# All matmuls as 64-row halves in pairs, the convolution in the h ring, turns through SyncE

## The chip, the cores and the metric

The kernel runs on one core of a Trainium2 chip. The metric is device time in microseconds of one execution, lower is better. The engines of the core work side by side, each through its own instructions in order: TensorE (PE) for matmuls, ScalarE (ACT), VectorE (DVE), GpSimd (POOL), and SyncE (SP), which issues most of the DMAs. They wait for each other by semaphores. TensorE writes into PSUM, eight banks of 2 KB per partition; ACT and DVE read it from there.

## The reference

A causal convolution of 7 taps, one softmaxed filter per head of 24 channels, and then a two-layer network with the gate h·cos(h):

```python
w = softmax(weight, axis=-1)                      # [8 heads, 7 taps]
x_pad = zeros(6 tokens) + x                       # x: [8, 4096, 192] float32
out[b,s,h,g] = sum_k w[h,k] * x_pad[b, s+k, h, g]  # 8 heads x 24 channels
x = out.reshape(32768, 192)
h = x @ w_in                                      # [192, 2048]
g = h * cos(h)
return g @ w_out                                  # [2048, 192], float32
```

## The kernel before

The 32768 tokens are worked in 64 tiles `t` of T = 512 tokens; two tiles make a unit `u` of 1024 tokens, the grain of loading, convolution and transposing. All matmuls take bf16 and sum in float32.

Per unit: `load_unit` loads x (SP's DMA queue), `cast_unit` makes it bf16 on POOL, with the block before it in front. `conv_pair` makes the convolution on PE, tokens on the 128 partitions: for each head, one matmul with a 128x128 band of filter taps on the block itself and one on the block before. `conv_out` copies the result to `ct` on ACT. `turn_unit` doubles 64 of the 192 channels on POOL, so that they later stand on both halves of the partitions, and transposes `ct` into `cT` (channels on partitions) by a DMA that SP issues, `dma_start_transpose`.

Per tile there are NP = 8 stages `j`. In stage `j`, `mm1(t, j)` makes 256 of the 2048 hidden features in a tile `h` of two PSUM banks. The contraction of 192 is 128 + 64: two matmuls of 64 rows (`w2`, one on the upper and one on the lower half of the rows, each to its own bank, line 184) and two of 128 rows (`w1`, line 187). ACT takes sin(h + pi/2) into `cs` (line 189) and DVE multiplies `h` by `cs` into `g` (line 192). Then `mm2(t - 1, j)` makes a part of the output of the tile before: 8 of the 64 matmuls `g` times `wo` that the tile needs, of 128 rows and 192 columns (line 204). After every second 128-token block ACT copies `o_ps` to `o_sb` (line 207) and after the fourth SP issues the store (line 209).

There is no scheduler: each engine runs its instructions in the order in which the loops write them (`manual_schedule`). The convolution of the next unit stands in stages 0, 2, 4 and 6 of the even tiles, and `turn_unit`, `load_unit` and `cast_unit` in stage 0 of the odd ones. PSUM: three `h` tiles (six banks), one bank for `o_ps`, one for `c_ps`.

Of the kernel before, what the change touches and what calls it, by code (L numbers as in the profile page):

```python
# [8 lines left out]
FP32 = mybir.dt.float32  # L9
BF16 = mybir.dt.bfloat16  # L10
AF = mybir.ActivationFunctionType
ALU = mybir.AluOpType
PSUM = bass.MemoryType.PSUM
# [3 lines left out]
def kernel(  # L17
# [8 lines left out]
    nc = tc.nc  # L26
    B, S, D = x.shape
    H, K = weight.shape
    Dff = moe_w_in.shape[1]
    G = D // H  # L30
    NTOK = B * S
    T = 512
    NT = NTOK // T
    NB = T // 128
    U = 1024
    NU = NTOK // U
    UB = U // 128
    UPS = S // U
    TPU = U // T
    NF = Dff // 128  # L40
    NP = NF // 2
# [4 lines left out]
    consts = ctx.enter_context(tc.tile_pool(name="consts", bufs=1))  # L46
# [5 lines left out]
    cos_pool = ctx.enter_context(tc.tile_pool(name="cos", bufs=3))  # L52
    gpool = ctx.enter_context(tc.tile_pool(name="g", bufs=2))
    opool = ctx.enter_context(tc.tile_pool(name="o", bufs=2))
    h_pool = ctx.enter_context(tc.tile_pool(name="h_ps", bufs=3, space=PSUM))
    o_pool = ctx.enter_context(tc.tile_pool(name="o_ps", bufs=1, space=PSUM))
    c_pool = ctx.enter_context(tc.tile_pool(name="c_ps", bufs=1, space=PSUM))

    ctx.enter_context(tc.manual_schedule())

# [6 lines left out]
    def load_unit(u):  # L67
        xt = xin.tile([128, UB, D], FP32, name="x_f")
        nc.sync.dma_start(out=xt, in_=xf[u * U : (u + 1) * U, :].rearrange("(n p) d -> p n d", p=128))
        x_tiles[u] = xt  # L70
# [14 lines left out]
    row = consts.tile([H, LR], BF16)  # L85
# [18 lines left out]
    band = consts.tile([128, H, 256], BF16)  # L104
    nc.vector.tensor_copy(out=band, in_=skew[:, :, ::-1])  # L105

    halfpi = consts.tile([128, 1], FP32)
    nc.vector.memset(halfpi, math.pi / 2.0)  # L108

    w1 = consts.tile([128, Dff], BF16)  # L110
    w2 = consts.tile([128, NP, 128], BF16)
    wo = consts.tile([128, NF, D], BF16)


    prev = {}
    bf = {}

    def cast_unit(u):
        xt = x_tiles.pop(u)
        xb = xbf_pool.tile([128, UB + 1, D], BF16, name="x_bf")  # L120
        if u % UPS == 0:
            nc.gpsimd.memset(xb[:, 0, :], 0.0)  # L122
        else:
            nc.gpsimd.tensor_copy(out=xb[:, 0, :], in_=bf[u - 1][:, UB, :])  # L124
        nc.gpsimd.tensor_copy(out=xb[:, 1 : UB + 1, :], in_=xt)  # L125
        bf[u] = xb
        bf.pop(u - 2, None)

    ct_tiles = {}

    def conv_pair(u, q):

        xb = bf[u]
        if q == 0:
            ct_tiles[u] = ct_pool.tile([128, UB, 256], BF16, name="ct")
        ct = ct_tiles[u]
        ps = c_pool.tile([128, 2, UB, G], FP32, name="c_ps")
        for i in range(2):
            h = 2 * q + i
            hs = slice(h * G, (h + 1) * G)  # L140
            nc.tensor.matmul(out=ps[:, i], lhsT=band[:, h, 0:128], rhs=xb[:, 1 : UB + 1, hs], start=True, stop=False)  # L141
            nc.tensor.matmul(out=ps[:, i], lhsT=band[:, h, 128:256], rhs=xb[:, 0:UB, hs], start=False, stop=True)  # L142
        return ct, ps

    def conv_out(q, ct, ps):
        o = ct[:, :, 2 * q * G : (2 * q + 2) * G].rearrange("p n (i g) -> p i n g", i=2)
        nc.scalar.copy(o, ps)  # L147

    cT = {}

    def turn_unit(u):
        ct = ct_tiles.pop(u)
        nc.gpsimd.tensor_copy(out=ct[:, :, D:256], in_=ct[:, :, 128:D])  # L153
        t = cT_pool.tile([128, UB, 2, 128], BF16, name="cT")
        nc.sync.dma_start_transpose(out=t.rearrange("p n c k -> p (n c) k"), in_=ct.rearrange("p n k -> p (n k)"))
        cT[u] = t
        cT.pop(u - 2, None)

    def conv_unit(u):
        for q in range(H // 2):  # L160
            conv_out(q, *conv_pair(u, q))
        turn_unit(u)

    cast_unit(0)
    nc.gpsimd.tensor_copy(out=w2, in_=w2_f)  # L165
    nc.vector.tensor_copy(out=w1, in_=w1_f)
    conv_unit(0)
    cast_unit(1)
    for q in range(4):
# [3 lines left out]
    g_tiles = {}  # L173
    o_state = {}

    def mm1(t, j):

        c = cT[t // TPU]
        n0 = (t % TPU) * NB
        x1 = c[:, n0 : n0 + NB, 0, :]  # L180
        h = h_pool.tile([128, 2, T], FP32, name="h")
        for i in range(2):
            r = slice(64 * i, 64 * i + 64)
            nc.tensor.matmul(out=h[:, i, :], lhsT=w2[r, j, :], rhs=c[r, n0 : n0 + NB, 1, :], start=True, stop=False)  # L184
        for i in range(2):
            f = 2 * j + i
            nc.tensor.matmul(out=h[:, i, :], lhsT=w1[:, f * 128 : (f + 1) * 128], rhs=x1, start=False, stop=True)  # L187
        cs = cos_pool.tile([128, 2, T], BF16, name="cs")
        nc.scalar.activation(out=cs, in_=h, func=AF.Sin, bias=halfpi, scale=1.0)  # L189
        if j == 0:  # L190
            g_tiles[t] = gpool.tile([128, NF, T], BF16, name="g")
        nc.vector.tensor_tensor(out=g_tiles[t][:, 2 * j : 2 * j + 2, :], in0=h, in1=cs, op=ALU.mult)  # L192

    def mm2(t, j):

        g = g_tiles[t]
        s, half = divmod(j, 2)
        if s % 2 == 0 and half == 0:
            o_state["ps"] = o_pool.tile([128, 2, 256], FP32, name="o_ps")
        if j == 0:  # L200
            o_state["sb"] = opool.tile([128, NB, D], FP32, name="o_sb")
        ps, sb = o_state["ps"], o_state["sb"]
        for f in range(half * 8, half * 8 + 8):
            nc.tensor.matmul(out=ps[:, s % 2, 0:D], lhsT=g[:, f, s * 128 : (s + 1) * 128], rhs=wo[:, f, :],  # L204
                             start=(f == 0), stop=(f == NF - 1))
        if s % 2 == 1 and half == 1:
            nc.scalar.copy(sb[:, s - 1 : s + 1, :], ps[:, :, 0:D])  # L207
            if s == NB - 1:
                nc.sync.dma_start(out=out[t * T : (t + 1) * T, :].rearrange("(n p) d -> p n d", p=128), in_=sb)

    for t in range(NT + 1):
        u_next = t // TPU + 1
        for j in range(NP):
            if t < NT:
                mm1(t, j)
                if u_next < NU:
                    k = (t % TPU) * NP + j
                    if k < H and k % 2 == 0:
                        conv_out(k // 2, *conv_pair(u_next, k // 2))
                    if k == H:  # L220
                        turn_unit(u_next)
                        if u_next + 1 < NU:
                            load_unit(u_next + 1)
                            cast_unit(u_next + 1)
            if t > 0:
                mm2(t - 1, j)


# [28 lines left out]
```

## Time and profile before

| | |
|---|---|
| time, median of 3 runs | 874.5 us (874.49 to 874.55) |
| the profiled execution | 874.82 us, span 873.0 us, granted clock 1.0 |
| PE matmuls of 64 rows, `h`, L184 | 1024 x 388 ns |
| PE matmuls of 128 rows, `h`, L187 | 1024 x 385 ns |
| PE matmuls, `o_ps`, L204 | 4096 x 246 ns |
| ACT sine L189, copies L147 and L207 | 512 x 1114 ns, 128 x 472 ns, 128 x 472 ns |
| DVE multiply L192 | 512 x 1225 ns |
| POOL cast L125, halo copy L124, doubling L153 | 1468 ns, 350 ns, 616 ns |
| x load and transpose, issue to landing | 4.9 us, 5.0 us |

A line of the groups names the source line, the engine, the operation, what is written and read, its count, and then the busy time, the mean of one instruction in ns, and the idle time before them with what ended it. A matmul's recorded time runs from its start to the end of its way through the array, so records of one stream overlap: the interval between starts tells what a matmul costs in a stream. In a timeline each row has the start, the time covered, the engine and what ran; neighbours of one kind are merged (x8).

### The profile page before, as it was taken

The numbers are of one execution on the slowest core, as the hardware profiler recorded it, in microseconds if no ns is written. First come the engines' busy times: TensorE is split into PE (matmuls) and PEld (weight loads), VectorE is DVE, ScalarE is ACT, GpSimd is POOL, SyncE is SP. The second block draws the span as 40 slices with busy tenths as digits, with TensorE's granted clock in tenths as the row PEclk, the third lists the DMA queues.
The fourth block names the chain that finished last, engine by engine and source line by source line (L and its number), as shares of the span: only waits on it lengthen the run. The fifth ranks groups of instructions, "written<-read, shape, count | busy, mean of one in ns | idle before, by whom it ended". The sixth has DMA issues, their size and how long they took to land.

```text
span 873.0 us, 15646 instructions
## 1 busy us (share of the span) xinstructions
PE 835.6 (96%) x6656; PEld 504.3 (58%) x6656; DVE 631.7 (72%) x525; ACT 668.0 (77%) x771; POOL 76.5 (9%) x101
## 2 busy tenths in 40 slices
PE   0699999999999999999999999999999999999997
PEld 0256566665656665556666566665656666556655
DVE  1477777777777777777777777777777777777774
ACT  0577878877778787778777778778777887777874
POOL 1101100101100101110101110100110110110000
PEclk9999999999999999999999999999999999999999
DMA  8133332133332133333134333124334223334201
GB/s 241 24 80 97 86 90 62 58 93 97 96 81 70 59 85 97 98 79 77 59 78 98 97 79 89 53 71 98 97 80 88 59 66 97 97 80 97 57 25 54
DMA packets 138038, 71.80 MB, mean 82 GB/s; under 512 B 68200, under 2 KB 137840, under 8 KB 137840
## 3 DMA queue, kind: packets, MB, share of 16 engines
q1 hardware_dynamic: 136896, 70.27, 31.5%
q8 instruction: 52, 0.85, 0.4%
q10 hardware_dynamic: 1072, 0.53, 0.2%
q14 instruction: 18, 0.15, 0.1%
HBM read 28.84 MB, written 25.17 MB: 62 GB/s over the span
## 4 chain that ended last, share of the span: by engine, by line
PE 84%; ACT 7%; issue 5%; DMA 2%; DVE 0%; POOL 0%; ACTq 0%
PE o_ps L204 35%; PE h L187 27%; PE h L184 16%; ACT o_sb L207 4%; ACT cs L189 3%; PE c_ps L141 3%; PE c_ps L142 2%; DMA skew<-row_d 1%; DMA row_d<-row 1%; DMA cT<-ct 0%; DVE g L192 0%; ACT ct L147 0%; DMA w_sb<-in_weight_dram 0%; ACT L91 0%; DVE band L105 0%
## 5 line engine op out<-in xcount | busy, mean ns | idle before, releaser
L192 DVE TENSOR_TENSOR g<-h,cs 128x1024 bf16<-128x1024 f32 x512 | 626.9, 1225 | 213.5 <-ACT cs L189 213.4
L189 ACT ACTIVATE cs<-h,halfpi 128x1024 bf16<-128x1024 f32 x512 | 570.1, 1114 | 173.5 <-PE h L187 169.0
L204 PE MATMUL o_ps<-wo,g 128*128 128x192 bf16 x4096 | 420.4, 246 | 4.9 <-ACT o_sb L207 1.5
L204 PEld LDWEIGHTS <-g 128*128 128x128 bf16 x4096 | 351.4, 98 | 106.7 <-issue 23.5
L187 PE MATMUL h<-cT,w 128*128 128x512 bf16 x1024 | 310.9, 385 | 0.0
L184 PE MATMUL h<-cT,w 64*128 64x512 bf16 x1024 | 200.5, 388 | 6.4 <-DMA cT<-ct 5.6
L187 PEld LDWEIGHTS <-w 128*128 128x128 bf16 x1024 | 57.9, 97 | 116.5 <-issue 116.5
L184 PEld LDWEIGHTS <-w 64*128 64x128 bf16 x1024 | 49.6, 93 | 88.6 <-issue 88.5
L147 ACT CAST ct<-c_ps 128x384 bf16<-128x384 f32 x128 | 60.4, 472 | 20.1 <-PE c_ps L142 20.1
L141 PE MATMUL c_ps<-x_bf,band 128*128 128x192 bf16 x256 | 53.8, 250 | 22.0 <-DVE halfpi L108 20.3
L125 POOL CAST x_bf<-x_f 128x1536 bf16<-128x1536 f32 x32 | 47.0, 1468 | 299.6 <-DMA x_f<-in_x_dram 299.6
L207 ACT COPY o_sb<-o_ps 128x384 f32<-128x384 f32 x128 | 60.4, 472 | 5.8 <-PE o_ps L204 5.8
L153 POOL COPY ct<-ct 128x512 bf16<-128x512 bf16 x32 | 19.7, 616 | 443.2 <-ACT ct L147 443.2
L142 PE MATMUL c_ps<-x_bf,band 128*128 128x192 bf16 x256 | 54.0, 251 | 0.0
L141 PEld LDWEIGHTS <-band 128*128 128x128 bf16 x256 | 25.6, 100 | 35.4 <-DVE halfpi L108 20.3
L142 PEld LDWEIGHTS <-band 128*128 128x128 bf16 x256 | 25.4, 99 | 17.3 <-issue 2.9
L105 DVE COPY band<-skew 128x2048 bf16<-128x2048 bf16 x1 | 0.7, 694 | 15.2 <-DMA skew<-row_d 15.2
L124 POOL COPY x_bf<-x_bf 128x192 bf16<-128x192 bf16 x24 | 8.4, 350 | 0.0
L91 ACT ACT_TABLE_LOAD x1 | 1.3, 1283 | 2.2 <-DMA w_sb<-in_weight_dram 2.2
L122 POOL MEMSET x_bf<- 128x192 bf16 x8 | 2.1, 259 | 0.3 <-POOLq L241 0.3
L170 DVE CAST wo<-wo_f 128x768 bf16<-128x768 f32 x4 | 2.0, 554 | 0.0
L165 POOL CAST w<-w_f 128x1024 bf16<-128x1024 f32 x1 | 1.0, 1042 | 4.0 <-DMA w_f<-in_moe_w_in_dram 4.0
(14 smaller groups left out, 4.3 us busy)
## 6 DMA issues: line engine op xcount, KB each, us to landing
x_f<-in_x_dram SPq DMA_DIRECT2D x32, 768.0 KB, 4.9
out_dram<-o_sb SPq DMA_DIRECT2D x64, 384.0 KB, 2.9
wo_f<-in_moe_w_out_dram SPq DMA_DIRECT2D x1, 1536.0 KB, 13.1
w_f<-in_moe_w_in_dram SPq DMA_DIRECT2D x1, 1024.0 KB, 7.5
w_f<-in_moe_w_in_dram SPq DMA_DIRECT2D x2, 256.0 KB, 8.4
skew<-row_d ACTq DMA_DIRECT2D x1, 512.0 KB, 9.3
cT<-ct SPq DMA_TRANSPOSE x32, 5.0
w_sb<-in_weight_dram ACTq DMA_DIRECT2D x1, 0.2 KB
```

What stands on the lines that cost most here:

```text
L124: nc.gpsimd.tensor_copy(out=xb[:, 0, :], in_=bf[u - 1][:, UB, :])
L125: nc.gpsimd.tensor_copy(out=xb[:, 1 : UB + 1, :], in_=xt)
L141: nc.tensor.matmul(out=ps[:, i], lhsT=band[:, h, 0:128], rhs=xb[:, 1 : UB + 1, hs], start=True, stop=False)
L142: nc.tensor.matmul(out=ps[:, i], lhsT=band[:, h, 128:256], rhs=xb[:, 0:UB, hs], start=False, stop=True)
L147: nc.scalar.copy(o, ps)
L153: nc.gpsimd.tensor_copy(out=ct[:, :, D:256], in_=ct[:, :, 128:D])
L184: nc.tensor.matmul(out=h[:, i, :], lhsT=w2[r, j, :], rhs=c[r, n0 : n0 + NB, 1, :], start=True, stop=False)
L187: nc.tensor.matmul(out=h[:, i, :], lhsT=w1[:, f * 128 : (f + 1) * 128], rhs=x1, start=False, stop=True)
L189: nc.scalar.activation(out=cs, in_=h, func=AF.Sin, bias=halfpi, scale=1.0)
L192: nc.vector.tensor_tensor(out=g_tiles[t][:, 2 * j : 2 * j + 2, :], in0=h, in1=cs, op=ALU.mult)
L204: nc.tensor.matmul(out=ps[:, s % 2, 0:D], lhsT=g[:, f, s * 128 : (s + 1) * 128], rhs=wo[:, f, :], start=(f == 0), stop=(f == NF - 1))
L207: nc.scalar.copy(sb[:, s - 1 : s + 1, :], ps[:, :, 0:D])
```

## The change

Every matmul becomes one or two of 64 rows (half the contraction), written in pairs: one on the upper row half, one on the lower, each into a bank of its own. As both halves of a contraction must end in the same bank, the halves swap banks in the middle. `Turn.mark` puts a no-op on SP that waits for the matmuls given to it, and `Turn.wait` makes later matmuls wait for that no-op.

- Hidden features: `first` (two pairs) and `last` (one pair, after the turn); between them stand 12 of the 16 output halves of the stage, or in stage 0 the first half of a convolution part. Tile 0 keeps the old form (`full`).
- Output: `o_ps` holds all four blocks of a tile in two banks; stages 0 to 3 write with the halves one way round, stages 4 to 7 the other way, with one turn between. One ACT copy per tile (line 284) takes it, placed before the sine of stage 7. The store of a tile is issued in stage 2, two tiles later.
- Convolution: `conv_part` makes four heads in 12 halves (four on the upper rows, eight on the lower; the block before needs the lower rows alone), in stage 0 of every tile, in a tile of the `h` ring in place of `c_ps`.
- In odd tiles POOL's doubling and the x load stand in stage 0, the transpose in stage 3, the cast in stage 4.
- The bias of the sine is an immediate number in place of a tile.

```diff
     opool = ctx.enter_context(tc.tile_pool(name="o", bufs=2))
     h_pool = ctx.enter_context(tc.tile_pool(name="h_ps", bufs=3, space=PSUM))
     o_pool = ctx.enter_context(tc.tile_pool(name="o_ps", bufs=1, space=PSUM))
-    c_pool = ctx.enter_context(tc.tile_pool(name="c_ps", bufs=1, space=PSUM))
 
     ctx.enter_context(tc.manual_schedule())
 
...
 
-    prev = {}
+    sync_dep = mybir.DependencyInfo(mybir.DependencyClass.Sync, mybir.DependencyReason.DATA)
+
+    class Turn:
+
+
+
+        def mark(self, *insts):
+            self.nop = nc.sync.nop()
+            for m in insts:
+                tc.add_manual_dep(self.nop.ins, m.ins.name, sync_dep, reason="row halves on one bank")
+
+        def wait(self, *insts):
+            for m in insts:
+                tc.add_manual_dep(m.ins, self.nop.ins.name, sync_dep, reason="row halves on one bank")
+
+    turn_o = Turn()
+
+
     bf = {}
 
     def cast_unit(u):
@@ -128,37 +141,60 @@
 
     ct_tiles = {}
 
-    def conv_pair(u, q):
+    def conv_part(u, c):
+
 
         xb = bf[u]
-        if q == 0:
+        ps = h_pool.tile([128, 2, T], FP32, name="h")
+
+        def mm(i, k, start=False):
+            h = 4 * c + i
+            rows = slice(0, 64) if k == 0 else slice(64, 128)
+            prev = k == 2
+            return nc.tensor.matmul(
+                out=ps[:, i // 2, (i % 2) * UB * G : (i % 2 + 1) * UB * G].rearrange("p (n g) -> p n g", g=G),
+                lhsT=band[rows, h, 128 if prev else 0 : 256 if prev else 128],
+                rhs=xb[rows, 0 if prev else 1 : UB if prev else UB + 1, h * G : (h + 1) * G],
+                start=start, stop=prev, skip_group_check=True)
+
+        mm(0, 0, True)
+        mm(2, 1, True)
+        up = mm(1, 0)
+        mm(2, 2)
+        mm(3, 2)
+        turn = Turn()
+        turn.mark(up, mm(3, 1))
+        yield
+        turn.wait(mm(0, 1))
+        mm(0, 2)
+        mm(1, 1)
+        turn.wait(mm(2, 0))
+        mm(1, 2)
+        mm(3, 0)
+        if c == 0:
             ct_tiles[u] = ct_pool.tile([128, UB, 256], BF16, name="ct")
+        o = ct_tiles[u][:, :, 4 * c * G : (4 * c + 4) * G].rearrange("p n (b i g) -> p b i n g", b=2, i=2)
+        for b in range(2):
+            nc.scalar.copy(o[:, b], ps[:, b, 0 : 2 * UB * G].rearrange("p (i n g) -> p i n g", i=2, n=UB))
+        yield
+
+    cT = {}
+
+    def double_unit(u):
         ct = ct_tiles[u]
-        ps = c_pool.tile([128, 2, UB, G], FP32, name="c_ps")
...
+        nc.gpsimd.tensor_copy(out=ct[:, :, D:256], in_=ct[:, :, 128:D])
 
     def turn_unit(u):
         ct = ct_tiles.pop(u)
-        nc.gpsimd.tensor_copy(out=ct[:, :, D:256], in_=ct[:, :, 128:D])
         t = cT_pool.tile([128, UB, 2, 128], BF16, name="cT")
         nc.sync.dma_start_transpose(out=t.rearrange("p n c k -> p (n c) k"), in_=ct.rearrange("p n k -> p (n k)"))
         cT[u] = t
         cT.pop(u - 2, None)
 
     def conv_unit(u):
-        for q in range(H // 2):
-            conv_out(q, *conv_pair(u, q))
+        for c in range(2):
+            list(conv_part(u, c))
+        double_unit(u)
         turn_unit(u)
 
     cast_unit(0)
@@ -173,57 +209,122 @@
     g_tiles = {}
     o_state = {}
 
-    def mm1(t, j):
...
+    class Hidden:
+
+
+        def __init__(self, t, j):
+            self.t, self.j = t, j
+            self.c = cT[t // TPU]
+            self.n0 = (t % TPU) * NB
+            self.h = h_pool.tile([128, 2, T], FP32, name="h")
+
+        def part(self, i, rows, w, c, start=False, stop=False):
+            return nc.tensor.matmul(out=self.h[:, i, :], lhsT=w, rhs=self.c[rows, self.n0 : self.n0 + NB, c, :],
+                             start=start, stop=stop)
+
+        def w1(self, i, rows):
+            f = 2 * self.j + i
+            return w1[rows, f * 128 : (f + 1) * 128]
+
+        def full(self):
+            for i in range(2):
+                r = slice(64 * i, 64 * i + 64)
+                self.part(i, r, w2[r, self.j, :], 1, start=True)
+            for i in range(2):
+                self.part(i, slice(0, 128), self.w1(i, slice(0, 128)), 0, stop=True)
+
+        def first(self):
+
+            up, lo = slice(0, 64), slice(64, 128)
+            self.part(0, up, self.w1(0, up), 0, start=True)
+            self.part(1, lo, self.w1(1, lo), 0, start=True)
+            self.turn = Turn()
+            self.turn.mark(self.part(0, up, w2[up, self.j, :], 1), self.part(1, lo, w2[lo, self.j, :], 1))
+
+        def last(self):
+
+            up, lo = slice(0, 64), slice(64, 128)
+            self.turn.wait(self.part(1, up, self.w1(1, up), 0, stop=True),
+                           self.part(0, lo, self.w1(0, lo), 0, stop=True))
+
+        def out(self):
+            cs = cos_pool.tile([128, 2, T], BF16, name="cs")
+            nc.scalar.activation(out=cs, in_=self.h, func=AF.Sin, bias=math.pi / 2.0, scale=1.0)
+            if self.j == 0:
+                g_tiles[self.t] = gpool.tile([128, NF, T], BF16, name="g")
+            nc.vector.tensor_tensor(out=g_tiles[self.t][:, 2 * self.j : 2 * self.j + 2, :], in0=self.h, in1=cs,
+                                    op=ALU.mult)
+
+    def mm2(t, j, lo, hi):
+
 
         g = g_tiles[t]
-        s, half = divmod(j, 2)
-        if s % 2 == 0 and half == 0:
-            o_state["ps"] = o_pool.tile([128, 2, 256], FP32, name="o_ps")
-        if j == 0:
+        if j == 0 and lo == 0:
+            o_state["ps"] = o_pool.tile([128, 2, T], FP32, name="o_ps")
             o_state["sb"] = opool.tile([128, NB, D], FP32, name="o_sb")
         ps, sb = o_state["ps"], o_state["sb"]
-        for f in range(half * 8, half * 8 + 8):
...
+        swap, j = divmod(j, 4)
+        fh, si = divmod(j, 2)
+        for k in range(lo, hi):
+            f = fh * 8 + k
+            for r in range(2):
+                b = r ^ swap
+                s = 2 * b + si
+                rows = slice(64 * r, 64 * r + 64)
+                m = nc.tensor.matmul(out=ps[:, b, si * D : (si + 1) * D], lhsT=g[rows, f, s * 128 : (s + 1) * 128],
+                                 rhs=wo[rows, f, :], start=(swap == 0 and f == 0 and si == 0),
+                                 stop=(swap == 1 and f == NF - 1), skip_group_check=True)
+                if swap and j == 0 and k == 0:
+                    turn_o.wait(m)
+                if swap == 0 and j == 3 and k == 7:
+                    if r == 1:
+                        turn_o.mark(o_state["m"], m)
+                    o_state["m"] = m
+        if swap == 1 and j == 3 and hi == 8:
+            nc.scalar.copy(sb.rearrange("p (b s) d -> p b (s d)", b=2), ps[:, :, 0 : 2 * D])
+            o_state[t] = sb
+
+    def store(t):
+        nc.sync.dma_start(out=out[t * T : (t + 1) * T, :].rearrange("(n p) d -> p n d", p=128), in_=o_state.pop(t))
 
     for t in range(NT + 1):
         u_next = t // TPU + 1
         for j in range(NP):
-            if t < NT:
...
+            hid = Hidden(t, j) if t < NT else None
+            conv = conv_part(u_next, t % TPU) if j == 0 and t < NT and u_next < NU else None
+            if t == 0:
+                hid.full()
+                if conv:
+                    list(conv)
+            elif hid is None:
+                mm2(t - 1, j, 0, 8)
+            else:
+                hid.first()
+                if conv:
+                    next(conv)
+                    hid.last()
+                    next(conv)
+                    mm2(t - 1, j, 0, 8)
+                else:
+                    mm2(t - 1, j, 0, 6)
+                    hid.last()
+                    mm2(t - 1, j, 6, 8)
+            if hid is not None:
+                hid.out()
+
+            if j == 2 and t > 1:
+                store(t - 2)
+            if t % TPU == TPU - 1 and u_next < NU:
+                if j == 0:
+                    double_unit(u_next)
+                if j == 3:
+                    turn_unit(u_next)
+                if u_next + 1 < NU:
+                    if j == 0:
+                        load_unit(u_next + 1)
+                    if j == 4:
+                        cast_unit(u_next + 1)
+    store(NT - 1)
 
 
 # ---- launch: one core; inputs and outputs as the reference has them ----
```

More of the change, by code (lines that the diff above doesn't have):

```diff
@@ L105 @@
     nc.vector.tensor_copy(out=band, in_=skew[:, :, ::-1])
-    halfpi = consts.tile([128, 1], FP32)
-    nc.vector.memset(halfpi, math.pi / 2.0)
     w1 = consts.tile([128, Dff], BF16)
@@ L129 @@
     ct_tiles = {}
-    def conv_pair(u, q):
+    def conv_part(u, c):
         xb = bf[u]
-        if q == 0:
-            ct_tiles[u] = ct_pool.tile([128, UB, 256], BF16, name="ct")
-        ct = ct_tiles[u]
-        ps = c_pool.tile([128, 2, UB, G], FP32, name="c_ps")
[L138 to L149, printed above, removed]
+        ps = h_pool.tile([128, 2, T], FP32, name="h")
[23 more added lines that the diff above has]
+        if c == 0:
+            ct_tiles[u] = ct_pool.tile([128, UB, 256], BF16, name="ct")
+        o = ct_tiles[u][:, :, 4 * c * G : (4 * c + 4) * G].rearrange("p n (b i g) -> p b i n g", b=2, i=2)
[4 more added lines that the diff above has]
+    def double_unit(u):
+        ct = ct_tiles[u]
+        nc.gpsimd.tensor_copy(out=ct[:, :, D:256], in_=ct[:, :, 128:D])
     def turn_unit(u):
         ct = ct_tiles.pop(u)
-        nc.gpsimd.tensor_copy(out=ct[:, :, D:256], in_=ct[:, :, 128:D])
         t = cT_pool.tile([128, UB, 2, 128], BF16, name="cT")
@@ L174 @@
     o_state = {}
-    def mm1(t, j):
[L178 to L189, printed above, removed]
-        if j == 0:
-            g_tiles[t] = gpool.tile([128, NF, T], BF16, name="g")
-        nc.vector.tensor_tensor(out=g_tiles[t][:, 2 * j : 2 * j + 2, :], in0=h, in1=cs, op=ALU.mult)
@@ L194, in mm2 @@
-    def mm2(t, j):
+    class Hidden:
[33 more added lines that the diff above has]
+                                    op=ALU.mult)
@@ L196, in mm2 @@
+    def mm2(t, j, lo, hi):
         g = g_tiles[t]
-        s, half = divmod(j, 2)
-        if s % 2 == 0 and half == 0:
-            o_state["ps"] = o_pool.tile([128, 2, 256], FP32, name="o_ps")
-        if j == 0:
+        if j == 0 and lo == 0:
+            o_state["ps"] = o_pool.tile([128, 2, T], FP32, name="o_ps")
             o_state["sb"] = opool.tile([128, NB, D], FP32, name="o_sb")
         ps, sb = o_state["ps"], o_state["sb"]
-        for f in range(half * 8, half * 8 + 8):
-            nc.tensor.matmul(out=ps[:, s % 2, 0:D], lhsT=g[:, f, s * 128 : (s + 1) * 128], rhs=wo[:, f, :],
-                             start=(f == 0), stop=(f == NF - 1))
@@ L206, in mm2 @@
[L206 to L209, printed above, removed]
+        swap, j = divmod(j, 4)
[15 more added lines that the diff above has]
+                    o_state["m"] = m
@@ L213 @@
         for j in range(NP):
-            if t < NT:
[L215 to L226, printed above, removed]
+            hid = Hidden(t, j) if t < NT else None
[32 more added lines that the diff above has]
+    store(NT - 1)
 _INS = ['x', 'weight', 'moe_w_in', 'moe_w_out']
```

## The prediction

> **What bounds the kernel now.** I read the page's first two parts and its chain first: is it one engine all the way, and is its clock whole?
>
> ```profile
> PE 835.6 (96%) x6656; PEld 504.3 (58%) x6656; DVE 631.7 (72%) x525; ACT 668.0 (77%) x771; POOL 76.5 (9%) x101
> PEclk9999999999999999999999999999999999999999
> PE 84%; ACT 7%; issue 5%; DMA 2%; DVE 0%; POOL 0%; ACTq 0%
> ```
>
> TensorE (PE) is busy 96% at full clock and carries the chain; ACT and DVE have a quarter to spare. But "busy" counts pipelined records, so I went to the timeline of PE for one stage, and for the convolution:
>
> ```profile
> 408.74 0.39 PE L184 MATMUL h<-cT,w 64*128 64x512 bf16 x2
> 409.06 0.60 PE L187 MATMUL h<-cT,w 128*128 128x512 bf16 x2
> 409.50 0.82 PE L204 MATMUL o_ps<-wo,g 128*128 128x192 bf16 x8
> 410.26 0.39 PE L184 MATMUL h<-cT,w 64*128 64x512 bf16 x2
> 410.58 0.60 PE L187 MATMUL h<-cT,w 128*128 128x512 bf16 x2
> ```
>
> ```profile
> 420.36 0.25 PE L141 MATMUL c_ps<-x_bf,band 128*128 128x192 bf16 x1
> 420.44 0.25 PE L142 MATMUL c_ps<-x_bf,band 128*128 128x192 bf16 x1
> 420.52 0.25 PE L141 MATMUL c_ps<-x_bf,band 128*128 128x192 bf16 x1
> 420.61 0.25 PE L142 MATMUL c_ps<-x_bf,band 128*128 128x192 bf16 x1
> 420.69 0.82 PE L204 MATMUL o_ps<-wo,g 128*128 128x192 bf16 x8
> ```
>
> First column start, second time covered. A stage repeats every 410.26 - 408.74 = 1.52 us. A 192-column matmul follows another every (420.69 - 420.36)/4 = 0.0825 us, two 512-column ones take 409.50 - 409.06 = 0.44 us (0.216 each, a little for the first). The two 64-row matmuls, of 0.388 us each in the groups, cover 0.39 us together: they run side by side, one slot of 0.216. So from 409.50 to 410.26 there are 8 x 0.0825 = 0.66 us of streaming and 0.10 of nothing; from 410.26 to 410.58, 0.216 and another 0.10. Each change between 128-row and 64-row matmuls costs about 0.10 us, 0.20 a stage.
>
> Then the groups, for durations, and the timeline of SP, because the change gives SP work:
>
> ```profile
> L192 DVE TENSOR_TENSOR g<-h,cs 128x1024 bf16<-128x1024 f32 x512 | 626.9, 1225 | 213.5 <-ACT cs L189 213.4
> L189 ACT ACTIVATE cs<-h,halfpi 128x1024 bf16<-128x1024 f32 x512 | 570.1, 1114 | 173.5 <-PE h L187 169.0
> L207 ACT COPY o_sb<-o_ps 128x384 f32<-128x384 f32 x128 | 60.4, 472 | 5.8 <-PE o_ps L204 5.8
> ```
>
> ```profile
> 407.96 0.37 SPq L209 DMA_DIRECT2D out_dram<-o_sb  x1
> 408.44 3.10 SPq L155 DMA_TRANSPOSE cT<-ct  x1
> 411.59 0.57 SPq L69 DMA_DIRECT2D x_f<-in_x_dram  x1
> 434.50 3.13 SPq L155 DMA_TRANSPOSE cT<-ct  x1
> 437.69 0.57 SPq L69 DMA_DIRECT2D x_f<-in_x_dram  x1
> ```
>
> The x load behind the transpose starts 411.59 - 408.44 - 3.10 = 0.05 us after it, in both units; the load has no row among SP's waits, so the queue alone held it. SP works in order and issuing a transpose occupies it for 3.1 us. Today nothing urgent stands behind it.
>
> **The sum, per unit of two tiles.** Sines eight stages apart give 26.07 us per unit, all through. 30 of the 32 are such units; the last, without convolution, takes 25.2, the first 23.2.
>
> Streaming that is left. A stage's hidden matmuls become three half-row pairs of 512 columns (as many slots as now), the eight output matmuls become eight pairs of 192: 3 x 0.216 + 8 x 0.0825 = 1.308 us. A convolution part is twelve halves, eight of them on the lower rows: 8 x 0.0825 = 0.66 us, what four heads cost now. Per unit 16 x 1.308 + 2 x 0.66 = 22.24 us. Against 26.07 this gives back 3.83: 3.2 of row changes, the rest small waits. It supposes that pairs follow each other at the interval of full matmuls with their weight loads hidden, which the trace shows for 128 rows only; the one 64-row pair always comes after a row change. Bounds: below nothing is excluded, since columns still stream one by one; nearest row 0, because full matmuls reload weights every 0.0825 us and the two 64-row loads cover 0.10 us together at a row change; the far row is an exposed load for each pair, the 0.0925 gap. I take 0 and keep the rest for a rival.
>
> The turn. After the hidden halves of `first`, an SP no-op waits for them and PE waits for the no-op before `last`. The second pair starts 0.216 into the stage and its records last 0.388: done at 0.60. From PE to ACT the trace needs 0.04, from DVE to PE 0.05, SP's next instruction 0.05, a weight load about 0.09: ready near 0.83. PE reaches `last` after 0.43 + 6 x 0.0825 = 0.93. Hidden, by 0.1 us; I take 0. Were a hop slower by 0.2, each of 14 stages would lose 0.1, 1.4 us a unit, 43 in all.
>
> Behind the transpose. It moves from stage 0 to stage 3 of odd tiles. In SP's order stand: the turn of stage 3, the output turn (ends with the last output matmul of stage 3), the transpose, the turn of stage 4. It so starts some 0.3 us into stage 4 (0.165 from stream to end of a matmul: 0.246 less 0.0825; then two hops), holds SP 3.1 us, and `last` gets its turn at about 3.55 instead of 0.93. PE stands 2.65 us. Output matmuls 7 and 8 and all later stages are queued behind that wait, and nothing makes it up: ACT and DVE only run dry. Lower end 0, if a no-op could pass a transpose; upper 3.1. The row of the x load decides: 2.65. The store (0.37, stage 2) and load (0.57, stage 0) precede a turn that is a stage away: 0. The cast on POOL (1.47 + 0.35, now at stage 4) has the rest of the tile; the x data land 4.9 us after an issue four stages earlier. The transposed tile lands 5.0 us after issue; four stages and the stall make 7.9: 0.
>
> The tile's seam. `o_ps` now holds a whole tile, so one ACT copy of 768 columns ends each tile instead of two of 384 (estimate from 472 ns for 384 and 1114 for 1024: 0.857 us), and in ACT's order it stands ahead of the sine of stage 7, which was ready before. The convolution takes a buffer of the `h` ring, so in the built program the first matmul of stage 1 waits for the multiply of stage 7 of the tile before. From the end of streaming: 0.165 + 0.04 + 0.857 + 0.035 + 1.114 + 0.03 + 1.225 + 0.05 = 3.52 us. PE's own work in between is stage 0 with its part, 1.308 + 0.66 = 1.97. It waits 1.55, two times a unit 3.1. Inside this lie the wait of the convolution for the ring and for its own turn. Bounds: the copy could be 0.47 or 1.1, the seam 1.2 to 1.8. Later stages: from `first` over sine and multiply back to the ring is 3.9 us for three buffers, 1.29 a stage, just under 1.308: 0.
>
> The immediate bias removes a memset and a wait in the prologue and leaves a sine of the same elements: 0 either way, at most 0.05 on one sine per seam, 3 us.
>
> Sum: 22.24 + 2.65 + 3.1 = 27.99 against 26.07, +1.92 a unit. Thirty of them +57.6; the first, with one seam and one transpose, about +1.5; the last, with neither convolution nor transpose and a seam of about 0.9, 22.7 against 25.2, -2.5; the last copy +0.4. Together +57. The profiled execution took 874.8 us (span 873.0), 0.3 over the median of 874.5: 874.8 + 57 = 932.
>
> Two rules of the skill bear on this. The Trainium skill, "TensorE: Matmul & The Clock Gate", Part 1, has the clock fall to half after an idle window of about 3.4 us. Here the granted clock is full in every slice; a stand of 2.65 stays under that window, so by the rule too nothing is added, but if a stand grew past it the next matmuls would run at half speed. The same page, Part 2, speaks against doubling matmuls: without hardware decode a matmul costs about 62 ns of sequencer, so 22 in a stage would need 1.36 us in place of 1.308, up to 0.9 a unit, and the sum would be 932 to 960. No run here shows this: the densest row is one matmul per 82.5 ns.
>
> **The rivals.** Pairs are slower than full matmuls (issue, weight loads): each 10 ns on 192 pairs a unit is 1.9 us, of which some 0.5 hides in the seams: +44 us, 976; at 15 ns 998. Against it: two 64-row matmuls start together at the row change. Fully exposed, 0.0925 on each, it would be above 1300; and if the halves ran one behind the other, the change not doing what it says, PE needs 44.5 us a unit and the time is past 1400.
>
> On the other side: the turns do not queue behind the transpose, because its 3.1 us is not SP's own time. Then 25.34 a unit, -0.73, and with the ends about 874.8 - 25 = 850. It decides as soon as less than some 0.7 us of the 2.65 remains. Against it stands the x load, held 0.05 us after each transpose. If the seam hid as well, 22.24 a unit gives about 757; I see no cover for it.
>
> **How the numbers follow.** Turns behind the transpose with the seam: 0.63, 915 to 955 by the bounds of seam and turn. Pairs slower by 5 to 15 ns or late turns, with the rest as above: 0.18, 955 to 1005. Much slower pairs or serial halves: 0.07. Turns free of the transpose: 0.10, with 0.02 in it for a hidden seam. About no change, by a mix: 0.02. The range 905 to 1005 leaves out the last three. A measurement of this kernel can tell 0.2% (1.7 us) from no change. Slower 0.63 + 0.18 + 0.07 = 0.88, same 0.02, faster 0.10.
>
> **What would show it.** In the profile after: no 0.10 us gaps around the 512-column matmuls; output pairs every 0.0825 us; once per unit a stand of PE near 2.65 us before a `last` whose release is SP's turn, with the transpose in SP's timeline through it; once per tile some 1.5 us before stage 1, released by DVE; an output copy of about 0.86 us on ACT with a sine right behind. Wrong would be: `last` starting while the transpose is still on SP; pairs spaced by much over 83 ns; a stall in every stage instead of one; a clock below full.

## The result, and the profile after

The changed kernel takes 888.1 us in the median (885.5 to 891.4) against 874.5 in the same runs: 1.016 times the time before, interval 1.012 to 1.020. It is slower, as forecast, but by 14 us and not by 57. The profiled execution took 885.45 us, with a span of 883.7.

The page's first part:

```profile
PE 751.2 (85%) x12016; PEld 535.3 (61%) x12016; DVE 631.0 (71%) x524; ACT 620.6 (70%) x707; POOL 76.3 (9%) x101
```

PE went from 96% to 85% of a longer span: it has less to do and waits more. Its three largest waits outside the prologue (total us, times, longest):

```profile
PE h L222 <- SPq L118: 42.7, 31, 2.5
PE h L154 <- DVE g L255: 28.8, 61, 0.5
PE h L222 <- DVE g L255: 27.9, 63, 2.4
```

L118 is the no-op of a turn: 31 waits, one for each transpose but the first. The other two are the seam, 61 to 63 times: the convolution waits for the multiply of stage 6, stage 1 for that of stage 7. A stretch in which PE does nothing is called a stand. PE's timeline around one transpose, and then SP's:

```profile
418.63 0.68 PE L274 MATMUL o_ps<-wo,g 64*128 64x192 bf16 x12
419.12 0.40 PE L222 MATMUL h<-cT,w 64*128 64x512 bf16 x2
419.34 0.34 PE L274 MATMUL o_ps<-wo,g 64*128 64x192 bf16 x4
419.50 0.61 PE L222 MATMUL h<-cT,w 64*128 64x512 bf16 x4
419.94 0.67 PE L274 MATMUL o_ps<-wo,g 64*128 64x192 bf16 x12
421.68 0.39 PE L222 MATMUL h<-cT,w 64*128 64x512 bf16 x2 [1.07 <-SPq L118]
```

```profile
417.66 0.38 SPq L288 DMA_DIRECT2D out_dram<-o_sb  x1
419.85 1.72 SPq L190 DMA_TRANSPOSE cT<-ct  x1
```

Stage 3 runs from `first` to `last` without a hole: 12 output halves between 418.63 and 419.12 are six pairs of 0.082 us, and there is no gap at the 512-column matmuls any more. In stage 4 `last` starts at 421.68, 0.11 us after SP is done with the transpose (419.85 + 1.72). But the transpose held SP for 1.72 us here (the median over the run is 1.92), where the kernel before showed 3.1.

The seam on ACT and DVE, between two tiles:

```profile
412.55 0.80 ACT L284 COPY o_sb<-o_ps 128x768 f32<-128x768 f32 x1 [0.45 <-PE o_ps L274]
413.24 1.03 ACT L252 ACTIVATE cs<-h 128x1024 bf16<-128x1024 f32 x1
414.31 1.23 DVE L255 TENSOR_TENSOR g<-h,cs 128x1024 bf16<-128x1024 f32 x1 [0.95 <-ACT cs L252]
415.58 0.61 PE L222 MATMUL h<-cT,w 64*128 64x512 bf16 x4 [0.41 <-DVE g L255]
```

Copy, sine, multiply, stage 1: the chain of the prediction, in its order. It is shorter than worked out, because the sine is:

```profile
L252 ACT ACTIVATE cs<-h 128x1024 bf16<-128x1024 f32 x512 | 525.2, 1026 | 176.5 <-PE h L222 176.4
```

1026 ns where it was 1114. By sines eight stages apart, an even tile takes 12.36 us (median), an odd one, with the transpose, 13.90.

### The profile page after: what moved, and what is told of

Same layout as the page of the kernel before. It is cut to its first block, busy times and chain, and to the rows that moved or that the text cites. A ratio compares the mean times of both kernels' runs of the same rounds, so it can differ in the third digit from the quotient of the medians.

```text
span 883.7 us, 26935 instructions
## 1 busy us (share of the span) xinstructions
PE 751.2 (85%) x12016; PEld 535.3 (61%) x12016; DVE 631.0 (71%) x524; ACT 620.6 (70%) x707; POOL 76.3 (9%) x101
## 3 DMA queue, kind: packets, MB, share of 16 engines
q8 instruction: 94, 1.54, 0.7%
## 4 chain that ended last, share of the span: by engine, by line
issue 82%; POOL 8%; PE 6%; DMA 2%; ACT 1%; DVE 1%; SPq 0%; POOLq 0%; ACTq 0%
POOL x_bf L138 5%; PE o_ps L274 3%; PE h L222 2%; POOL ct L185 2%; DMA skew<-row_d 1%; POOL x_bf L137 1%; DMA row_d<-row 1%; DVE g L255 1%; PE h L154 0%; SPq L190 0%; ACT o_sb L284 0%; ACT cs L252 0%; POOL x_bf L135 0%; DMA w_sb<-in_weight_dram 0%; ACT L90 0%
## 5 line engine op out<-in xcount | busy, mean ns | idle before, releaser
L252 ACT ACTIVATE cs<-h 128x1024 bf16<-128x1024 f32 x512 | 525.2, 1026 | 176.5 <-PE h L222 176.4
L222 PE MATMUL h<-cT,w 64*128 64x512 bf16 x3056 | 520.0, 378 | 76.6 <-SPq L118 42.7
L274 PE MATMUL o_ps<-wo,g 64*128 64x192 bf16 x8192 | 514.5, 243 | 2.1 <-ACT o_sb L284 1.8
L274 PEld LDWEIGHTS <-g 64*128 64x128 bf16 x8192 | 395.6, 94 | 145.6 <-SPq L118 10.1
L222 PEld LDWEIGHTS <-w 64*128 64x128 bf16 x3056 | 160.0, 94 | 105.0 <-issue 55.1
L154 PE MATMUL h<-x_bf,band 64*128 64x192 bf16 x768 | 66.1, 250 | 49.3 <-DVE g L255 28.8
L154 PEld LDWEIGHTS <-band 64*128 64x128 bf16 x768 | 39.3, 95 | 93.2 <-DVE g L255 29.0
L178 ACT CAST ct<-h 128x384 bf16<-128x384 f32 x128 | 55.0, 482 | 47.2 <-PE h L154 37.4
L284 ACT COPY o_sb<-o_ps 128x768 f32<-128x768 f32 x64 | 51.1, 798 | 33.6 <-PE o_ps L274 33.6
```

The source lines that it names most:

```text
L154: return nc.tensor.matmul(out=ps[:, i // 2, (i % 2) * UB * G : (i % 2 + 1) * UB * G].rearrange("p (n g) -> p n g", g=G), lhsT=band[rows, h ...
L178: nc.scalar.copy(o[:, b], ps[:, b, 0 : 2 * UB * G].rearrange("p (i n g) -> p i n g", i=2, n=UB))
L222: return nc.tensor.matmul(out=self.h[:, i, :], lhsT=w, rhs=self.c[rows, self.n0 : self.n0 + NB, c, :], start=start, stop=stop)
L252: nc.scalar.activation(out=cs, in_=self.h, func=AF.Sin, bias=math.pi / 2.0, scale=1.0)
L274: m = nc.tensor.matmul(out=ps[:, b, si * D : (si + 1) * D], lhsT=g[rows, f, s * 128 : (s + 1) * 128], rhs=wo[rows, f, :], start=(swap == 0 ...
L284: nc.scalar.copy(sb.rearrange("p (b s) d -> p b (s d)", b=2), ps[:, :, 0 : 2 * D])
```

## The experiments

e4 and e6 to e10 are single runs, the others the median of four to seven.

**Where does the transpose stand on SP?** Theory: the turn queues behind it. Rival: PE's stand has another cause. Two kernels move the transpose alone in the changed kernel, the second in two halves.

```diff
-                if j == 3:
+                if j == 4:
                     turn_unit(u_next)
```

> Only the transpose moves, from stage 3 to stage 4 of odd tiles, so that it stands right behind the turn of stage 4 and no longer behind the output turn. Theory (the turn of the next stage queues behind the transpose on SP): a transpose of 1.9 us now starts about 0.7 us into its stage instead of at its end; the next turn is due 1.2 us later, so PE stands about 0.7 us per unit instead of 1.4. Time 885 - 31 x 0.7 = about 863. Rival (the stand of PE comes from something else, so the place of the transpose in SP's order does not matter): about 885 as before.

Measured: 859.1 us, 0.982 of the kernel before (0.980 to 0.984). The wait for the turn fell from 42.7 to 17.1 us in total:

```profile
PE h L222 <- SPq L118: 17.1, 29, 1.8
```

```diff
-                if j == 3:
-                    turn_unit(u_next)
+                if j == 1:
+                    turn_half(u_next, 0)   # blocks 0 to 3 of cT
+                if j == 4:
+                    turn_half(u_next, 1)   # blocks 4 to 7
```

> The transpose is issued as two halves, in stages 1 and 4 of odd tiles, each right behind a turn. Theory: each half holds SP about 1 us, which fits between two turns (1.2 us), so no stand of PE is left behind it: 31 x 1.38 = 43 us less, 842 or somewhat below, odd tiles as short as even ones (12.4 us), and a full clock all through since no stand of 2 us is left. Rival: half a transpose costs SP as much as a whole one, then two stands of 0.7 us, about 885.

Measured: 840.1 us, 0.960 (0.959 to 0.961). PE's wait for the turn and SP's timeline:

```profile
PE h L229 <- SPq L118: 3.6, 5, 1.0
421.87 1.23 SPq L193 DMA_TRANSPOSE cT<-ct  x1
423.22 0.51 SPq L295 DMA_DIRECT2D out_dram<-o_sb  x1
425.73 1.23 SPq L193 DMA_TRANSPOSE cT<-ct  x1
```

31 waits became 5. Half a transpose holds SP for 1.23 us, not for 1.0, which still fits between two turns. Odd tiles fell to 12.45 us beside 12.35. The theory holds: the place of the transpose on SP alone was worth 29 us (e1), its place and its split into two halves 48 us.

**Why 1.9 us and not 3.1?** Theory: a transpose is held longer when a store was issued on the queue just before it. The first test puts the store ahead of the transpose in the changed kernel, the second was to take it away from there in the kernel before.

```diff
-            if j == 2 and t > 1:
+            if j == (3 if t % TPU == TPU - 1 else 2) and t > 1:
                 store(t - 2)
```

> In odd tiles the store is issued right ahead of the transpose, as in the kernel before, instead of a stage earlier. Theory A (a transpose issued while the packets of a store are under way takes 3.1 us of SP, else 1.9): the transpose takes 3.1 us, the stand of PE grows from 1.4 to about 2.7 plus the 0.4 of the store, time about 930. Theory B (the 3.1 us came from something else in the kernel before): transposes stay at 1.9 us, time about 897 by the store's 0.38 us alone.

```profile
PE h L222 <- SPq L118: 93.7, 31, 3.9
423.89 0.38 SPq L288 DMA_DIRECT2D out_dram<-o_sb  x1
424.38 3.23 SPq L190 DMA_TRANSPOSE cT<-ct  x1
```

Measured: 958.6 us, median transpose 3.14 us, PE's wait for the turn more than doubled. That is theory A, and more than its 930: the odd tile has 15.7 us instead of 13.9 (31 x 1.8 = 56), and 13 times in the run the clock fell to half after such a stand, 12 times for 3.4 us and once for 6.8.

```diff
-                    if k == H:
+                    if k == H + 2:
                         turn_unit(u_next)
```

> The kernel before with turn_unit, load_unit and cast_unit two stages later, so that the transpose is not issued right behind the store. Theory (a store under way makes the transpose hold SP for 3.1 us): the transpose takes about 1.9 us here; time 874.5 as before, since nothing urgent stands behind it. Rival (3.1 us belongs to that kernel for another reason): 3.1 us.

Measured: 875.1 us and 3.12 us. This tested nothing: in the kernel before nothing on SP ties the transpose to PE's stage, so SP still issued it 0.48 us after the store. Changing its place relative to the store takes a change of SP's order:

```diff
+            if j == 1 and t > 1:
+                store(t - 2)        # behind the transpose; no longer at the end of mm2
```

> The kernel before with the store of a tile issued in stage 1 two tiles later, so that on SP it stands behind the transpose and no longer right ahead of it. (e7 moved the transpose in the program, but SP had nothing to wait for in between and issued it behind the store all the same.) Theory (a store just issued on the same queue makes the transpose hold SP for 3.1 us): the transpose takes about 1.9 us; time as before within 0.3%. Rival (3.1 us for another reason): 3.1 us.

```profile
407.22 1.78 SPq L155 DMA_TRANSPOSE cT<-ct  x1
409.06 1.10 SPq L69 DMA_DIRECT2D x_f<-in_x_dram  x1
```

Measured: 875.3 us, and a median of 1.85 us. The same instruction in the same kernel takes 3.1 us right behind the store and 1.85 without; now the load behind the transpose takes 1.1 us where it took 0.57. The store has to stand right ahead: in the changed kernel it is issued some 2.2 us before the transpose and in all thirty cases had not landed when the transpose began, and the median is still 1.92 us. What the store does to the transpose no run shows.

**The seam.** The copy of `o_ps` moves behind the sine of stage 7, all else as in the changed kernel.

```diff
             if hid is not None:
                 hid.out()
+            if j == NP - 1 and t > 0:
+                take(t - 1)         # the copy of o_ps, taken out of mm2
```

> The copy of o_ps stands behind the sine of stage 7 in ACT's order instead of ahead of it. Theory (the seam is the chain copy, sine, multiply, first matmul of stage 1): the chain loses the copy, about 0.7 us; PE's wait before stage 1 (0.41 us a tile) goes, the wait of the convolution for the multiply of stage 6 stays. 25 us less, about 860. Rival (the output matmuls of the next tile then wait for the copy): PE gains a wait of the same size before the output matmuls of stage 0, time 880 to 890.

Measured: 866.7 us, 0.991 (0.989 to 0.994). PE's waits for the turn and before stage 1:

```profile
PE h L222 <- SPq L118: 48.1, 31, 2.7
PE h L222 <- DVE g L255: 2.6, 4, 1.8
```

The even tile went from 12.36 to 11.86 us, so the wait before stage 1 is gone and none took its place in the tile. 63 tiles shorter by 0.5 would be 31 us; the gain is 21, because the wait for the turn grew by 5.4 us and the profiled execution has four stretches at half clock behind long stands where the changed kernel has one in mid-run, each worth at most 1.7 us.

**The sine.** The kernel before with the immediate bias alone.

```diff
-        nc.scalar.activation(out=cs, in_=h, func=AF.Sin, bias=halfpi, scale=1.0)
+        nc.scalar.activation(out=cs, in_=h, func=AF.Sin, bias=math.pi / 2.0, scale=1.0)
```

> The kernel before with the immediate bias alone. Theory (the immediate bias is what took the sine from 1114 to 1023 ns): sine 1023 ns here too, and the time stays at 874.5 within 0.2%, since PE binds. Rival (the sine is shorter because of what runs beside it in the changed kernel): sine 1114 ns.

```profile
L186 ACT ACTIVATE cs<-h 128x1024 bf16<-128x1024 f32 x512 | 523.7, 1023 | 212.9 <-PE h L184 196.9
```

The sine takes 1023 ns here too: it is the bias. The time did not stay: 868.0 us, 6.7 less than the kernel before beside it (874.7). PE did not bind alone, as the same place of the two timelines shows, first the kernel before, then this one:

```profile
413.62 0.60 PE L187 MATMUL h<-cT,w 128*128 128x512 bf16 x2
413.76 0.47 ACT L207 COPY o_sb<-o_ps 128x384 f32<-128x384 f32 x1
414.28 0.82 PE L204 MATMUL o_ps<-wo,g 128*128 128x192 bf16 x8
```

```profile
410.31 0.60 PE L184 MATMUL h<-cT,w 128*128 128x512 bf16 x2
410.35 0.47 ACT L204 COPY o_sb<-o_ps 128x384 f32<-128x384 f32 x1
410.87 0.82 PE L201 MATMUL o_ps<-wo,g 128*128 128x192 bf16 x8
```

Output matmuls follow 0.66 and 0.56 us after the hidden ones, where 0.44 is the rule: they start 0.05 us after the end of the copy of `o_ps`, which stands on ACT behind a sine. Twice a unit 0.1 us: the unit fell from 26.07 to 25.88. Thirty such units make 5.5 of the 6.7 us; another 1.1 lies in the first unit (23.18 to 22.12).

And the counterpart, the halves of e2 with the tile bias:

> e2_transpose_halves with the bias of the sine taken from a tile again, as in the kernel before. Theory (the operand of the bias costs the sine 0.09 us and the sine stands in the chain of the seam): sine 1114 ns, even tiles 12.44 instead of 12.35 us, 840 + 63 x 0.09 = about 846. Rival (the sine is not in the chain that ends last): 1114 ns and 840.

```profile
L262 ACT ACTIVATE cs<-h,halfpi 128x1024 bf16<-128x1024 f32 x512 | 571.1, 1116 | 95.8 <-PE h L232 95.4 <-DVE g L265 0.4
```

Measured: 844.3 us, sine 1116 ns, even tile 12.44 us where e2 had 12.35. The sine stands in the seam's chain at full length.

**The row changes.** The changed kernel with `full` in all tiles in place of `first` and `last`; the outputs stay in 64-row pairs.

```diff
             else:
-                hid.first()
...
+                hid.full()
+                if conv:
+                    list(conv)
+                mm2(t - 1, j, 0, 8)
```

> The changed kernel with the hidden matmuls of every tile in the old form (two of 64 rows, two of 128), without first, last and their turns; the output matmuls stay in 64-row pairs, so the rows change twice a stage again. Theory (a row change costs 0.10 us): a stage is 1.51 us in place of 1.31, nothing stands behind the transpose, a unit is 16 x 1.51 + 1.32 + two seams of about 0.9 = 27.3 us, about 913. Rival (the gaps of the kernel before came from something else, such as the 128-row weight loads): stages of about 1.31 us, 850 or less.

```profile
423.18 0.92 PE L222 MATMUL h<-cT,w 64*128 64x512 bf16 x4
424.03 0.83 PE L274 MATMUL o_ps<-wo,g 64*128 64x192 bf16 x16
424.70 0.92 PE L222 MATMUL h<-cT,w 64*128 64x512 bf16 x4
```

A stage is 424.70 - 423.18 = 1.52 us again, as in the kernel before, and 1.31 without row changes. From 423.18 to 424.03 there are three slots of 0.216 and 0.20 of nothing. Part of it has moved along with the row change: from the output pairs to the 64-row hidden pair there is no gap now (424.70 - 424.03 = 0.67, eight pairs of 0.082), where the kernel before had 0.10 between them. What in a row change takes the time, the load of 128-row weights among others, these runs do not separate. The time is 928.9 us, above the 913, because a tile has about 1.0 us of seam in place of 0.9 and the convolution's turn now stands open.

**Both edits together**, the halves and the sine ahead of the copy:

> Both edits together on the changed kernel: the transpose in halves behind the turns of stages 1 and 4, and the copy of o_ps behind the sine of stage 7. Theory (two separate stands of PE): the gains add. The halves alone gave 840; the other order took the even tile from 12.36 to 11.86 us, so 2 x 0.5 us a unit, 31 us less: about 810, odd and even tiles near 11.9 us, full clock. Rival (with the transpose gone ACT or DVE binds, which have 10.7 and 9.8 us of work a tile): the tile stays above 12.2 us and the time above 830.

Measured: 816.1 us, 0.933 (0.931 to 0.935), even tile 11.86 us, odd 12.10. The even tile is as short as expected, the odd one keeps 0.24 us more; ACT, for which the rival counted 10.7 us a tile, is busy for 9.7. Then the first half goes to stage 2 and the store to stage 5:

> e5_halves_and_sine_first with the first half of the transpose in stage 2 instead of 1 and the store in stage 5 instead of 2. In e5 the first half waited for POOL's doubling, held SP until 2.1 us into its stage, the store stood right behind it, and the turn of stage 2 came 0.24 us late. Theory: that wait goes, odd tiles as even ones 11.86 us, 816 - 31 x 0.24 = about 808. Rival (the odd tile is longer for another reason): 816.

Measured: 809.6 us, 0.924 (0.922 to 0.926), odd tile 11.90. This version beats both kernels. Of PE's larger waits after the start, the convolution's for the multiply of stage 6 is left:

```profile
PE h L154 <- DVE g L262: 28.7, 61, 0.5
```

## Why the prediction was right or wrong

**Streaming, right.** 1.31 us a stage and pairs every 0.082 us were measured; e8 puts the 0.20 us of a stage on the row changes. The rival of slower pairs is out. The 62 ns of sequencer for each matmul that the prediction takes from the Trainium skill ("TensorE: Matmul & The Clock Gate", Part 2) did not show in any stage; but the 188 matmuls of a tile would need 11.66 us by it, just under the 11.86 of the shortest tile here, so no run excludes it.

**The turn, right:** hidden in every stage but the one behind the transpose.

**Behind the transpose: right mechanism, wrong size.** This is the first step that failed, and the costliest: the 2.65 us of the sum. I took the 3.1 us from the row of the kernel before. That row contained the store right ahead of it, and the change itself moves the store away, to stage 2. I costed the moved store at 0 by the time it holds SP, and did not ask what it does to the transpose behind it. Measured: 1.9 us of SP; PE's starts around the stand are 1.62 us apart on average where 0.08 is the rule, a stand of 1.54 instead of 2.65. e4 restores the 3.1 us, e10 takes it away from the kernel before. That kernel's trace held a warning: its first two transposes, before any store, take 1.86 and 1.32 us.

**The seam: right chain, too long.** 1.55 expected; 12.36 less the streaming of 8 x 1.308 + 0.66 = 11.12 leaves 1.24. The sine is 0.09 shorter, the copy 0.06 (0.798 for 0.857, which was drawn in part from a sine), and the sine starts 0.10 before the record of the copy ends (413.24 against 412.55 + 0.80), where 0.035 after it was counted. The second step that failed is the sentence on the immediate bias, "0 either way": it is 0.09 us on every sine, and e6 shows that it alone brings 6.7 us to the kernel before. There I had called 0.63 us a unit (3.83 less 3.2) "small waits" without looking who ended them.

**The sum.** Per unit 27.99 was expected and 26.42 measured, on average over 29 units: 29 x 1.57 = 46 us, nearly the whole distance from 932 to the profiled 885. The transpose gave 1.11 less and the seams 0.62; some 0.16 came back, of which the one half-speed stretch in mid-run is at most 0.06. That the sign came out as forecast was close: with streaming of 22.24 and seams of 2.48, a stand of 26.07 - 24.72 = 1.35 us would have made about no change, and 1.54 remained.

**The clock, wrong.** I held a stand below 3.4 us to be free, with the rule of the Trainium skill ("TensorE: Matmul & The Clock Gate", Part 1). Around the stand that ended at 791.52 PE shows:

```profile
788.62 0.68 PE L274 MATMUL o_ps<-wo,g 64*128 64x192 bf16 x12
791.52 0.44 PE L222 MATMUL h<-cT,w 64*128 64x512 bf16 x2 [2.22 <-SPq L118]
792.93 1.17 PE L274 MATMUL o_ps<-wo,g 64*128 64x192 bf16 x12
```

The same 12 matmuls cover 0.68 us before and 1.17 after: half clock, for 3.4 us, after 2.2 us of idleness. Behind other stands of 2.2 to 2.5 us it did not happen. Their place decides: in every trace the clock changes on a raster with steps of 3.413 us. Here are the step of this stand and the one after it, then the two steps over which a stand of 2.46 us fell (366.92 to 369.38). Before the comma stands the length of the step, behind it PE's busy time; the 1.00 or 0.50 near the end of each line is the granted clock.

```profile
788.31:791.73 3.42, 1.20 (x20) 0.66 (x16) 2.12 (x2) 0.95 (x1) 0.68 (x1) 1.00 0.77 93
791.73:795.14 3.41, 3.41 (x32) 2.17 (x30) 1.23 (x1) 1.60 (x2) 0.00 (x0) 0.50 0.37 83
365.06:368.48 3.42, 1.86 (x36) 1.30 (x30) 2.92 (x3) 1.54 (x2) 1.47 (x1) 1.00 0.85 145
368.48:371.89 3.41, 2.51 (x42) 1.80 (x44) 1.02 (x1) 1.79 (x2) 0.00 (x0) 1.00 0.52 115
```

The first step was idle for 65%, the other two for 46% and 26%. In all the traces, prologue and end left aside, the clock fell 24 times; 23 times the step before had been idle for 59% (2.0 us) or more, once for 54% (the start of e8). Of the steps without a fall one was idle for 60% (in e4) and none of the rest for more than 57%. The spread of the changed kernel, 885 to 891, goes with mean clocks of 0.996 to 0.992; e2, without such stands, stays within 839.6 and 840.5. So the measurement decides: the stand that suffices is shorter than the window, about 2.0 us where it falls within one step.

**The rival on the other side** did not occur as put (e1, e2 and e4 show the turns do queue), but it named the right lever: e2 is that kernel, 840 where the rival said 850.

## What to carry to other kernels

A semaphore turn through a DMA-issuing engine waits for whatever that engine is issuing ahead of it, so long instructions belong right behind a turn, in pieces shorter than the time to the next one. The duration of a DMA instruction belongs to its place in the queue as much as to itself: when a change moves its neighbour, the old row is a bound and not a price. And no small wait should be left unnamed when the change shortens the instruction that ends it.

## What the runs showed of the hardware beyond that

- Issuing a transpose holds SP for 1.85 to 1.92 us in the median, 3.1 us right behind a store of 384 KB, and 1.23 us for half of it. In the changed kernel single ones took up to 3.1 us without a store right ahead. All eight of 2.35 us or more ran while a 16 KB packet of the DMA queue that the page calls "instruction" was under way; of the other 24, at most 2.10 us, three did. That this packet is the cause was not tested.
- A sine of 128x1024 takes 1023 to 1026 ns with an immediate bias, 1114 to 1116 ns with one from a tile.
- Pairs of 64-row matmuls with new weights each time run at the rate of full matmuls, 0.082 us for 192 columns.
- PE's clock fell to half for a step of a 3.413 us raster (once for two) after steps in which PE had been idle for 59% or more; stands of 2.2 us within one step sufficed (the changed kernel, 791.52), one of 2.46 us across two did not (369.38).
